# Two hand-over terms and a new table of priority shifts in a kernel's own list scheduler

## The chip, the cores and the metric

The kernel runs on one NeuronCore of a Trainium2 chip. That core has a matrix engine (TensorE, PE in the profile, with its weight loads as PEld), a vector engine (VectorE, DVE), a scalar engine (ScalarE, ACT), GpSimd (POOL) and SyncE (SP), whose queue issues the loads from HBM. The engines run their own instruction streams in order and wait for each other by semaphores. The metric is the device time of one execution in microseconds; the kernel before takes 958.61 us, the median of three runs (958.48 to 958.99).

## The reference

Three stages follow each other. `q`, `k` and `v` are 4 × 8 × 576 × 64 (batch, heads, sequence, width); the tokens are 2304 rows of 512.

```python
# attention: two softmax attentions, summed
q_d, k_d, v_d = (mean over 4 neighbouring positions of q, k, v)   # 144 positions
out_d = softmax(scale * q_d @ k_d.T) @ v_d                         # then each row repeated 4 times
attn  = softmax(where(|i - j| < 4, scale * q @ k.T, -1e9))         # a band of 7 keys
x     = out_up + attn @ v                                          # -> (2304, 512)
# moe
h = x @ w_in                                # 512 -> 2048
g = maximum(h, 0) + alpha * minimum(h, 0)
x = g @ w_out                               # 2048 -> 512
# moe2
xn  = x / sqrt(mean(x*x) + 1e-6) * rms_g
g   = xn @ w_gate                           # 512 -> 1536
out = (g * sigmoid(g) * (xn @ w_val)) @ w_out2   # 1536 -> 512
```

Weights and `alpha`, `rms_g` arrive as float64, that is as pairs of 32-bit words.

## The kernel before, in words

**Products.** Every float32 factor of the large products is split into two float16 parts, `split` (L414): ScalarE writes the high part (L415), VectorE the low part (L416), after scaling with powers of two. A product is three float16 matmuls.

**Weights.** A `Piece` is a part of a weight. For each of its two halves SyncE loads the word pairs into a tile `wr` (L1143 for `w_in`, L1153 for `w_out`; a half of `w_in` is 768 KB), and `decode` (L1158) makes float32 of it: ScalarE works on the high words (L1162) and, for some pieces, on the low words (L1165), and VectorE joins them into `wc` or `wo` (L1167, or L1170 and L1171). `square` takes sums of squares on TensorE (L1183 `sqps`) and VectorE (L1184); from those of the first three pieces of `w_in`, six halves, `scale_in` makes the scale `swi` by a sum over the partitions (L391 `allps`) and some small steps. Only then can the first `wi<-wc,swi` (L415), a split of `w_in`, run, and the first product of the MoE after it.

**Batch 0's attention**, class `Dense`, works on four pairs of heads. `load` (L788) issues q and k of a head pair, two DMAs each (L795), 144 KB apiece; `loadv` (L803) and `vwin` (L815) bring v. `tr` transposes q and k on TensorE (L844 `tps`), ScalarE copies the result to `T` (L845; `T_185`, `T_190`, `T_200` and `T_205` are the head pairs 0 to 3), VectorE adds up neighbours (L847). `down` is the downsampled attention (scores L867, exponentials L877, transposes L895, copies `aT` L896, product L904, copies `outd` L909), `local` the banded one in thirds of the sequence ("lanes" 0, 1, 2): scores L920 to L932, exponentials L952, their normalizing L959 to L967, transposes L976 with copies `laT` L978, product L988, and a split to `xt`, the MoE's input. Lane 0 must be through before the MoE starts; lanes 1 and 2 run beside it.

**The first MoE product.** `m1_first` takes lanes 0, 1, 2 (192 columns each) over 16 blocks of `w_in` in pairs: `h_mm` (L1409) multiplies (L1416 `hps`), ScalarE takes the negative part (L1420 `g`), VectorE applies alpha (L1422), and the result is split (L415 and L416 with `g<-hps,sc`). Lane 0 also splits `w_in` on the way, so ScalarE has much to do there. Lane 1's attention and the decoding of `w_out` are woven between these steps. The remaining 700 us are long rows of matmuls: `acc` (L1433), `gps` (L1533), `oacc` (L1562).

**The order.** `issue_order` (L56) sets each engine's order. It holds a model of the machine: `cost` and `transfer` give durations, `lag` the delay from the end of an instruction to the start of one that needs it, and a flag `slow` says whether TensorE runs at half clock at that point of the model. A list scheduler, run 40 times backward and forward, gives each instruction a priority `lead`. Then every entry of `LEADS`, (from, to, shift in ns), shifts the priorities of a range of instruction numbers; a last forward run with these gives the order, which is fixed by `add_manual_dep`. The DMAs go out on one queue of SyncE, in its order.

## Time and profile before

| | |
|---|---|
| median of the runs | 958.61 us |
| the profiled execution's own time | 958.69 us |
| its span in the profile | 957.0 us |
| TensorE busy | 928.3 us, 97% |
| VectorE busy | 676.8 us, 71% |
| ScalarE busy | 481.4 us, 50% |
| GpSimd busy | 128.0 us, 13% |
| moved by DMA | 73.79 MB, mean 77 GB/s |

The span runs from the first to the last instruction that the profiler sees, and some 1.7 us of the execution lie around it. TensorE is busy nearly throughout; its idle time lies almost all in the first 100 us. In that part the other engines and the loads have their densest work.

### The profile page before, as it was taken

How to read it: one execution, taken by the hardware profiler on the slowest of the kernel's cores; microseconds unless marked ns; L12 is line 12 of the kernel's file. 1: busy time of each engine (PE TensorE's matmuls, PEld its weight loads, DVE VectorE, ACT ScalarE, POOL GpSimd, SP SyncE). 2: the span in 40 equal slices, each digit the busy share in tenths (PEclk: the TensorE clock that was granted, in tenths of full speed). 3: DMA queues.
4: the chain of work that ended last, by engine and by line, in shares of the span. 5: the costliest groups of instructions: out<-in, count | busy, mean ns of one | idle time of the engine just before them, and what ended most of it. 6: DMA issues, size and time to landing. Idle time of an engine off the chain costs nothing.

```text
span 957.0 us, 16449 instructions
## 1 busy us (share of the span) xinstructions
PE 928.3 (97%) x6484; PEld 599.6 (63%) x6484; DVE 676.8 (71%) x1333; ACT 481.4 (50%) x1108; POOL 128.0 (13%) x103
## 2 busy tenths in 40 slices
PE   6978999999999999999999999999999999999998
PEld 5667877799555565556666655555566666555554
DVE  4789996899999968999977899973333342442333
ACT  5899989889872472233576322222332433221322
POOL 1101100211022003332102323220000000000000
PEclk9999999999999999999999999999999999999999
DMA  9976444574221241121032120200000000000000
GB/s 214 278 253 177 130 143 130 196 234 137 72 74 58 91 150 50 55 78 55 25 88 84 50 65 20 50 18 1 23 12 1 1 2 1 1 1 12 23 1 34
DMA packets 53711, 73.79 MB, mean 77 GB/s; under 512 B 22190, under 2 KB 35138, under 8 KB 53634
## 3 DMA queue, kind: packets, MB, share of 16 engines
q1 hardware_dynamic: 53634, 72.74, 25.3%
q8 instruction: 51, 0.84, 0.4%
q14 instruction: 26, 0.21, 0.1%
HBM read 68.01 MB, written 4.72 MB: 76 GB/s over the span
## 4 chain that ended last, share of the span: by engine, by line
PE 78%; ACT 4%; DMA 3%; DVE 3%; issue 1%; SPq 0%; ACTq 0%
PE gps L1533 26%; PE acc L1433 16%; PE hps L1416 16%; PE oacc L1562 14%; DMA out_dram<-ob 3%; PE avps L749 1%; PE sps L709 1%; PE atps L737 1%; DMA wr<-in_moe_w_gate_dram 1%; ACT wr L1165 1%; ACT w L415 1%; DVE prod L575 1%; PE xps L612 1%; DVE hps L1422 1%; DVE wc L1167 0%
## 5 line engine op out<-in xcount | busy, mean ns | idle before, releaser
L1416 PE MATMUL hps<-xt,wi 128*128 128x192 f16 (+1 forms) x1536 | 345.9, 289 | 6.6 <-DVE g L416 4.3
L1533 PE MATMUL gps<-x,w 128*128 128x384 f16 x1728 | 349.5, 326 | 0.6 <-ACT x L1447 0.4
L1433 PE MATMUL acc<-ghl,wo 128*128 128x384 f16 (+1 forms) x960 | 249.4, 310 | 0.5 <-ACT ghl L415 0.4
L1533 PEld LDWEIGHTS <-w 128*128 128x128 f16 x1728 | 169.4, 98 | 116.5 <-issue 2.6
L1562 PE MATMUL oacc<-w,uhl 128*128 128x512 f16 x630 | 200.4, 379 | 1.8 <-ACT ob L1618 1.7
L1416 PEld LDWEIGHTS <-wi 128*128 128x128 f16 x1536 | 148.0, 100 | 59.3 <-issue 7.7
L1433 PEld LDWEIGHTS <-wo 128*128 128x128 f16 x1344 | 128.8, 99 | 60.0 <-issue 2.6
L1422 DVE SCALAR_TENSOR_TENSOR hps<-g,oma,hps 128x192 f32<-128x192 f32 (+1 forms) x128 | 66.1, 517 | 66.1 <-ACT g L1420 65.4
L1542 ACT ACTIVATE th<-gps,tsc 128x384 f32<-128x384 f32 x72 | 41.7, 581 | 124.2 <-PE gps L1533 123.9
L1562 PEld LDWEIGHTS <-uhl 128*128 128x128 f16 x630 | 61.8, 98 | 64.3 <-issue 2.5
L1544 DVE SCALAR_TENSOR_TENSOR th<-th,gps 128x384 f32<-128x384 f32 x72 | 39.6, 551 | 84.9 <-ACT th L1542 84.7
L1553 ACT ACTIVATE uhl<-gps 128x384 f16<-128x384 f32 x72 | 41.7, 579 | 107.0 <-DVE gps L1547 98.5
L1420 ACT ACTIVATE g<-hps 128x384 f32<-128x384 f32 x96 | 47.0, 489 | 95.7 <-PE hps L1416 95.4
L521 POOL TENSOR_TENSOR prod<-cq,ckv 128x896 f32<-128x896 f32 x24 | 53.1, 2213 | 172.9 <-DVE ls L532 52.2
L1433 PE MATMUL acc<-g,wo 128*128 128x384 f16 (+1 forms) x384 | 69.8, 286 | 0.0
L1554 DVE TENSOR_TENSOR uhl<-gps,uhl 128x384 f16<-128x384 f32 x72 | 45.4, 630 | 28.4 <-ACT uhl L1553 28.1
L575 POOL TENSOR_TENSOR prod<-ls,ckv 128x896 f32<-128x896 f32 x24 | 47.9, 1997 | 126.4 <-issue 54.8
L416 DVE SCALAR_TENSOR_TENSOR ghl<-hps,grp,ghl 128x384 f16<-128x384 f32 (+1 forms) x73 | 44.3, 608 | 27.0 <-ACT ghl L415 26.7
L415 ACT ACTIVATE ghl<-hps,grp 128x384 f16<-128x384 f32 (+1 forms) x73 | 41.9, 574 | 40.2 <-DVE hps L1422 37.2
L532 DVE TENSOR_REDUCE ls<-prod 128x14 f32<-128x896 f32 x48 | 51.0, 1076 | 0.0
L1162 ACT ACTIVATE wr<-wr 128x768 f32<-128x768 f32 (+1 forms) x48 | 41.5, 874 | 8.7 <-DMA wr<-in_moe_w_val_dram 4.9
L1547 DVE SCALAR_TENSOR_TENSOR gps<-th,kap,gps 128x384 f32<-128x384 f32 x60 | 37.1, 618 | 9.6 <-PE gps L1533 7.0
(240 smaller groups left out, 1143.4 us busy)
## 6 DMA issues: line engine op xcount, KB each, us to landing
wr<-in_moe_w_out_dram SPq DMA_DIRECT2D x18, 512.0 KB
wr<-in_moe_w_in_dram SPq DMA_DIRECT2D x10, 768.0 KB
wr<-in_moe_w_gate_dram SPq DMA_DIRECT2D x8, 768.0 KB
wr<-in_moe_w_val_dram SPq DMA_DIRECT2D x8, 768.0 KB
ckv<-in_k_dram SPq DMA_DIRECT2D x7, 768.0 KB
ckv<-in_v_dram SPq DMA_DIRECT2D x7, 768.0 KB
wr<-in_moe_w_out_dram SPq DMA_DIRECT2D x20, 256.0 KB
sd<-in_q_dram SPq DMA_DIRECT2D x24, 144.0 KB
```

The lines of the kernel that those rows point to most:

```text
L415: nc.scalar.activation(out=hi, in_=src, func=AF.Copy, scale=s)
L416: nc.vector.scalar_tensor_tensor(out=lo, in0=src, scalar=s, in1=hi, op0=ALU.mult, op1=ALU.subtract)
L521: engs[i].tensor_tensor(out=pr, in0=view(st["q"][:, j, t:t + TP], [[D, TP], [0, ND], [1, D]]), in1=view(st["k"][:, j, t:t + TP], [[D, TP], ...
L532: nc.vector.tensor_reduce(out=st["s"][:, j, t:t + TP], in_=st.pop(("p", i)), axis=AX.X, op=ALU.add)
L575: engs[i].tensor_tensor(out=over(pr, i), in0=view(st["s"][:, j, t:t + TP], [[ND, TP], [1, ND], [0, D]]), in1=view(st["v"][:, j, t:t + TP], ...
L1416: nc.tensor.matmul(ps[:, j], wi[:, f + j, a, kk * 128:(kk + 1) * 128], x[:, b_, kk, c0:c0 + n], start=(i == 0), stop=(i == 3 * KK - 1))
L1420: nc.scalar.activation(out=g, in_=ps, func=AF.Relu, scale=-1.0)
L1422: nc.vector.scalar_tensor_tensor(out=ps[:, j], in0=g[:, j], scalar=oma[:, f + j:f + j + 1], in1=ps[:, j], op0=ALU.mult, op1=ALU.add)
L1433: nc.tensor.matmul(acc[e], wo_f(f)[:, a, e * 128:(e + 1) * 128], hl[:, b_], start=(f == f0 and i == 0), stop=(f == f1 and i == 2))
L1533: nc.tensor.matmul(ps, w2_t[i0 + f // 3].rearrange("p a (k c) -> p a k c", k=KK)[:, a, kk, (f % 3) * 128:(f % 3 + 1) * 128], xh[:, b_, kk] ...
L1554: nc.vector.tensor_tensor(out=t1, in0=vp, in1=t0, op=ALU.subtract)
L1562: nc.tensor.matmul(acc[tt], t[:, a, tt * 128:(tt + 1) * 128], w[:, b_, f % 3], start=(f in first and i == 0), stop=(f in last and i == 2))
```

## The change

Three terms of the model change, and the table. In `transfer`, a load of at most 16 runs takes at least 3000 ns. In the forward run, while `slow` is set, a TensorE instruction that found its engine idle costs 90 ns more, and whatever waits for a TensorE instruction gets it 100 ns later (`late`). The table `LEADS` is another one, of 159 shifts in place of 164. No instruction is added or taken away on any engine: the two orders are permutations of the same instructions. Behind the changed lines all line numbers are larger by 3 (L845 becomes L848).

```diff
--- before.py
+++ after.py
@@ -22,34 +22,33 @@
 
 
 LEADS = (
-    (6142, 6149, 8500), (4634, 4657, 4000), (1841, 1850, 500), (2437, 2444, -500), (1116, 1482, 1000), (6896, 6972, -500),
...
+    (1516, 1525, -4500), (5545, 5548, 22500), (6896, 6972, -500), (6862, 6881, -3000), (3753, 3934, -5500), (1566, 1613, 500),
...
@@ -113,7 +112,7 @@
         n = max(runs(a)[0] for a in (o, i))
         each = 4.0 * min(runs(a)[1] for a in (o, i))
         share = n / 16 * (10.0 + 0.046 * each)
-        return max(share, n / rings * (9.0 + 0.042 * each)), max(share, 600.0)
+        return max(share, n / rings * (9.0 + 0.042 * each), 3000.0 if n <= 16 else 0.0), max(share, 600.0)
 
     def cost(k, ins, outs):
         i, e = insts[k], eng[k]
@@ -253,11 +252,15 @@
                 k = heapq.heappop(soon[e])[1]
                 heapq.heappush(now[e], (prio[k], k))
             k = heapq.heappop(now[e])[1]
+            late = 0.0
             if fwd and e == "PE":
                 while t >= (win + 1) * WIN:
                     slow, win, done = done < BUSY, win + 1, 0
                 done += work[k]
                 real[k] = (2 * d[k] - 2.5 if slow else d[k]) + fixed[k]
+                if slow:
+                    real[k] += 90.0 if t > clock[e] else 0.0
+                    late = 100.0
             if fwd and shared[k]:
                 real[k] += max(0.0, port - t)
                 port = t + real[k]
@@ -266,7 +269,7 @@
             seq[e].append(k)
             for s in S[k]:
                 left[s] -= 1
-                at[s] = max(at[s], end[k] + (lag(k, s) if fwd else lag(s, k)))
+                at[s] = max(at[s], end[k] + late + (lag(k, s) if fwd else lag(s, k)))
                 if not left[s]:
                     if fwd and mate.get(k) == s:
                         heapq.heappush(now[e], (-1e30, s))
```

What that does to the order, at three places.

SyncE's queue, from the sixth load of k to behind the last one. `wo<-in_q_dram` and `wo<-in_k_dram` are loads of batch 0's q and k, `wr<-in_moe_w_in_dram` a half of a piece of `w_in`, `sdv` and `vw` are v. Before:

```order
L795 DMA wo<-in_k_dram 96x6x64
L1143 DMA wr<-in_moe_w_in_dram 128x2x768
L795 DMA wo<-in_k_dram 96x6x64
L795 DMA wo<-in_q_dram 96x6x64
L815 DMA vw_186<-in_v_dram 93x64
L815 DMA vw_186<-in_v_dram 96x3x64
L1143 DMA wr<-in_moe_w_in_dram 128x2x768
L795 DMA wo<-in_k_dram 96x6x64
L815 DMA vw_186<-in_v_dram 6x4x64
L815 DMA vw_186<-in_v_dram 96x4x64
L815 DMA vw_186<-in_v_dram 6x4x64
L1143 DMA wr<-in_moe_w_in_dram 128x2x768
```

After:

```order
L798 DMA wo<-in_k_dram 96x6x64
L806 DMA sdv<-in_v_dram 72x2x512
L1146 DMA wr<-in_moe_w_in_dram 128x2x768
L798 DMA wo<-in_q_dram 96x6x64
L806 DMA sdv<-in_v_dram 72x2x512 x2
L1146 DMA wr<-in_moe_w_in_dram 128x2x768
L818 DMA vw_186<-in_v_dram 93x64
L798 DMA wo<-in_k_dram 96x6x64
L818 DMA vw_186<-in_v_dram 96x3x64
L818 DMA vw_186<-in_v_dram 6x4x64
L1146 DMA wr<-in_moe_w_in_dram 128x2x768
```

The last k load here is that of head pair 3. It had four halves of `w_in` ahead of it in the queue, two of them further up than these rows; now it has six, four of them further up, and these six are all that the first scale needs.

ScalarE, around the copies `T_205` of head pair 3 (`aT` and `laT` are copies of transposed probabilities, `dls` and `dd` probabilities). Before:

```order
L967 ACTIVATE dls<-dls,dlsum 96x102
L896 ACTIVATE aT<-atps 72x288
L1162 ACTIVATE wr<-wr 128x768
L967 ACTIVATE dls<-dls,dlsum 96x102
L1165 ACTIVATE wr<-wr,nhalf 128x768
L896 ACTIVATE aT<-atps 72x288 x2
L978 ACTIVATE laT<-ltps 102x384
L845 ACTIVATE T_205<-tps 128x288
L1162 ACTIVATE wr<-wr 128x768
L845 ACTIVATE T_205<-tps 128x288
L896 ACTIVATE aT<-atps 72x288
```

After:

```order
L970 ACTIVATE dls<-dls,dlsum 96x102 x6
L880 ACTIVATE dd,dsum<-sps,dm 72x144 x3
L970 ACTIVATE dls<-dls,dlsum 96x102
L880 ACTIVATE dd,dsum<-sps,dm 72x144
L848 ACTIVATE T_205<-tps 128x288 x2
L970 ACTIVATE dls<-dls,dlsum 96x102
L1165 ACTIVATE wr<-wr 128x768
L981 ACTIVATE laT<-ltps 102x384
L848 ACTIVATE T_205<-tps 128x288
L899 ACTIVATE aT<-atps 72x288
L848 ACTIVATE T_205<-tps 128x288
```

Before, the first three `aT` stood ahead of the first `T_205`; now the first comes behind three of the four. The transposes on TensorE that give `aT` (L895) moved in the same way: 22 small matmuls that stood ahead of the transposes of head pair 3's k, 16 of L895, four of L904, one each of L391 and L976, now stand behind.

ScalarE, up to the first split of `w_in` (`wi<-wc,swi`). Before:

```order
L415 ACTIVATE xt<-dxs,sc 128x192
L1165 ACTIVATE wr<-wr,nhalf 128x768
L978 ACTIVATE laT<-ltps 102x384
L1162 ACTIVATE wr<-wr 128x768
L1165 ACTIVATE wr<-wr,nhalf 128x768
L415 ACTIVATE xt<-dxs,sc 128x192
L1162 ACTIVATE wr<-wr 128x768
L415 ACTIVATE wi<-wc,swi 128x512 x9
L1162 ACTIVATE wr<-wr 128x768
L1420 ACTIVATE g<-hps 128x384
```

After:

```order
L418 ACTIVATE xt<-dxs,sc 128x192
L1165 ACTIVATE wr<-wr 128x768
L1168 ACTIVATE wr<-wr,nhalf 128x768
L418 ACTIVATE xt<-dxs,sc 128x192
L1165 ACTIVATE wr<-wr 128x256
L955 ACTIVATE dls,dlsum<-lsps,dlm 96x102 x14
L418 ACTIVATE wi<-wc,swi 128x512 x2
L955 ACTIVATE dls,dlsum<-lsps,dlm 96x102 x2
L418 ACTIVATE wi<-wc,swi 128x512 x4
L1165 ACTIVATE wr<-wr 128x768
```

Fourteen of the 16 exponentials of lane 1 (`dls,dlsum<-lsps`), of which thirteen stood behind the first nine splits and the rest further on, now stand ahead of the first split, and so do three decodes of high words of `w_out` (one 128x768, two 128x256), which stood behind it.

## Rows read from the trace of the kernel before

**Rows 1.** Busy time by stretch (start:end, length; per engine busy and instructions; PEclk; DMA; GB/s)
```profile
0.00:35.00 35.00, 25.89 (x161) 20.01 (x162) 19.71 (x67) 21.71 (x67) 4.67 (x29) 1.00 1.00 227
35.00:62.02 27.02, 25.37 (x199) 18.46 (x198) 20.51 (x48) 25.03 (x73) 2.43 (x2) 1.00 0.72 247
62.02:96.00 33.98, 27.32 (x294) 24.06 (x295) 31.84 (x77) 33.84 (x82) 3.99 (x8) 0.90 0.71 222
96.00:225.00 129.00, 127.71 (x1358) 107.23 (x1356) 113.79 (x272) 116.17 (x288) 16.55 (x13) 1.00 0.52 162
225.00:957.00 732.00, 721.98 (x4480) 429.86 (x4479) 490.93 (x872) 284.67 (x603) 100.33 (x52) 1.00 0.14 42
```

**Rows 2.** ScalarE's waits, 0 to 62.02 us (total us, times, longest us)
```profile
ACT T L845 <- PE tps L844: 9.9, 5, 5.5
ACT wr L1162 <- DMA wr<-in_moe_w_in_dram: 1.7, 1, 1.7
ACT aT L896 <- PE atps L895: 1.6, 4, 0.7
```

**Rows 3.** ScalarE by line and shape, 0 to 110 us (busy us, mean ns; idle before)
```profile
L1162 ACT ACTIVATE wr<-wr 128x768 f32<-128x768 f32 x20 | 18.1, 910 | 1.9 <-DMA wr<-in_moe_w_in_dram 1.7
L952 ACT ACTIVATE dls<-lsps,dlm 96x102 f32<-96x102 f32 x48 | 15.8, 343 | 0.3 <-DVE dlm L938 0.2
L1165 ACT ACTIVATE wr<-wr,nhalf 128x768 int32<-128x768 uint32 x14 | 14.0, 999 | 0.0
L415 ACT ACTIVATE wi<-wc,swi 128x512 f16<-128x512 f32 x16 | 10.5, 718 | 0.3 <-DVE swi L406 0.3
L978 ACT ACTIVATE laT<-ltps 102x384 f32<-102x384 f32 x8 | 3.8, 495 | 0.0
```

**Rows 4.** SyncE's queue in order of time (start us, us issuing)
```profile
25.86 1.36 SPq L795 DMA_DIRECT2D wo<-in_k_dram  x1
```

**Rows 5.** DMA, 0 to 36 us: rate in 40 slices, total, issues
```profile
GB/s 0 0 181 237 243 203 213 184 340 357 261 188 232 252 255 232 249 192 185 176 224 199 204 241 254 244 257 260 201 158 242 312 284 221 152 190 309 325 402 397
DMA packets 12547, 8.33 MB, mean 231 GB/s; under 512 B 10491, under 2 KB 10511, under 8 KB 12544
wr<-in_moe_w_in_dram SPq DMA_DIRECT2D x6, 768.0 KB
```

**Rows 6.** TensorE in order of time, 20 to 62 us (start us, us, idle before)
```profile
27.84 1.27 PE L895 MATMUL atps<-ident,dd 72*72 72x72 f32 x7
...
34.63 1.01 PE L844 MATMUL tps<-ident,wo 96*128 96x96 f32 x5
...
35.57 1.23 PE L904 MATMUL avps<-aT,dd 72*64 72x144 f32 x8
...
60.62 0.38 PE L391 MATMUL allps<-s,ones 128*128 128x3 f32 x2 [1.04 <-DVE sqps L1184]
```

**Rows 7.** ScalarE in order of time, 62.01 and 86 to 88 us
```profile
62.01 1.33 ACT L415 ACTIVATE wi<-wc,swi 128x512 f16<-128x512 f32 x2 [0.34 <-DVE swi L406]
...
86.71 0.49 ACT L1420 ACTIVATE g<-hps 128x384 f32<-128x384 f32 x1
87.08 0.59 ACT L415 ACTIVATE g<-hps,sc 128x384 f16<-128x384 f32 x1
```

**Rows 8.** TensorE in order of time, 88 to 94 us
```profile
88.38 0.57 PE L1416 MATMUL hps<-xt,wi 128*128 128x192 f16 x5 [0.16 <-DVE g L416]
...
89.05 0.55 PE L988 MATMUL lops<-laT,vw 102*64 102x96 f32 x8
...
93.63 0.60 PE L932 MATMUL lsps<-T 64*96 64x102 f32 x8
```

**Rows 9.** Busy time by stretch after the first weight split's start
```profile
64.40:67.80 3.40, 3.40 (x22) 3.13 (x23) 3.40 (x6) 3.26 (x7) 0.00 (x0) 0.50 1.02 382
74.70:78.10 3.40, 3.40 (x27) 3.26 (x25) 2.63 (x5) 3.40 (x16) 0.00 (x0) 0.50 0.98 292
...
88.40:125.00 36.60, 35.31 (x417) 29.28 (x417) 35.06 (x97) 34.20 (x109) 4.59 (x9) 1.00 0.48 136
```

53 rows, old and new, of the table LEADS are left out of this document.

## The prediction

> **What bounds the kernel now.** I read the table of stretches first. From 225 us to the end TensorE is busy for 722.0 of 732.0 us, from 96 to 225 us for 127.7 of 129.0 [rows 1]: there the kernel can't get shorter by order, save for a microsecond or two. The open time is ahead of 96 us: TensorE idles 9.1 us of the first 35, 1.7 of the next 27 and 6.7 of the 34 after that. So the question is by when the first 96 us have handed their work to TensorE, which from then on pays any lateness in full at the end.
>
> In those 96 us I then asked who is late. Between 62.02 and 96 us it is ScalarE: busy 33.84 of 33.98 us, while TensorE is at 27.3 [rows 1]. At 88.38 us the fifth pair of MoE products starts right behind VectorE's half of a split (0.16 us of idle), and that split ran on ScalarE at 87.08 us [rows 7, 8]: ScalarE, then VectorE, then TensorE. From 88.4 to 125 us TensorE still idles 1.3 us in all [rows 9]. So ScalarE's stream up to the split at 87.08 us sets the time, and everything ahead of it on ScalarE counts, work and idle time alike.
>
> Ahead of 62.02 us ScalarE is not full: it worked 21.7 + 25.0 = 46.7 us and idled 15.3. The waits name the reasons: copies of transposed q and k that wait for TensorE (9.9 us), the first word pairs of `w_in` (1.7 us), and copies of transposed probabilities (1.6 us) [rows 2]. The first split of `w_in` at 62.01 us waits only for its scale (0.34 us), which goes back to the sum over partitions on TensorE at 60.62 us [rows 6, 7].
>
> **What the change does, part by part.** Nothing is added or removed, so each price is one of place.
>
> *The new terms of the model* cost no time on the chip; only the order does.
>
> *The loads of q and k behind those of `w_in`.* Two more halves of 768 KB, together 2 × 0.786 = 1.57 MB, go out ahead of the last k. Its predecessors were issued until 25.86 us [rows 4], and TensorE transposed this k in the main at 34.63 us [rows 6]. At 231 GB/s, the mean of the first 36 us, the 1.57 MB take 6.8 us; at 402 GB/s, the best slice, 3.9 us [rows 5]. I take 5.0 us (317 GB/s, the middle of the two rates), since the loads of long rows stand among the short ones: of the packets in this stretch, 10491 of 12547 are under 512 B [rows 5]. TensorE shows no wait for this load now, so its cover is used up at 34.63 us and the delay counts whole: transposes at 39.6 us. The Trainium skill, "DMA: Bandwidth & Descriptors", section Specifications, puts the limit of HBM for one core at about 358 GB/s; the slices of 402 and 397 GB/s exceed it [rows 5]. By the page this term would be 4.4 us by estimate, 0.6 less.
>
> *22 small matmuls that stood ahead of those transposes stand behind them.* Sixteen of L895 at (1.27 − 0.33)/6 = 0.157 us each, 2.5 us; four of L904 at (1.23 − 0.46)/7 = 0.11, 0.4 us [rows 6] (0.33 and 0.46 are taken for the last one's length in such a row); two more at about 0.2. Together 3.4 us. If nothing else fills TensorE's wait for the load, they come on top of the delay; if they run in idle time that TensorE had anyhow, they are free. Both ends stay in the range; I take half, 1.7 us.
>
> *Up to the first split.* From TensorE's 34.63 us to the split at 62.01 us were 27.4 us, in which TensorE was busy for all but 1.7 of 27 [rows 1]; I keep that length. The split then comes at 39.6 + 27.4 + 1.7 = 68.7 us (67.0 to 70.4 by the matmuls alone, 65.9 to 72.2 with both ends of the rate).
>
> *Work that ScalarE now does ahead of the first split.* Fourteen exponentials of lane 1, at 15.8/48 = 0.33 us each, 4.6 us; one decode of 128x768, 18.1/20 = 0.9 us, and two of 128x256 at about half of it [rows 3]. That is 6.4 us by sums of busy time; as neighbours overlap by about 0.1 us (87.08 − 86.71 = 0.37 us between a start and the next where the first lasts 0.49 [rows 7]), I take 6.0. It falls into ScalarE's idle time as long as there is some: up to the split ScalarE has 46.7 + 6.0 = 52.7 us of work, so it idles 68.7 − 52.7 = 16.0 us, against 15.3 before. The cover of these 6 us is thus the wait for the scale; without the late loads the idle time would be down at 9.3 us, and that difference is the whole intended gain.
>
> *The balance at the split that was at 87.08 us.* Ahead of it ScalarE has, in the new order, four copies `laT` more (3.8/8 = 0.475 each, 1.9 us), four splits of `w_in` (10.5/16 = 0.656, 2.6), two decodes of low words (1.0 each) and half a one (0.5), one decode of high words and a half one (0.9 + 0.45), one split of `xt` (0.45), and one negative part less (0.49) [rows 3, 7]. That is 8.3 us by busy time; with the same overlap over some twelve instructions, 7.2. These 7.2 us contain the 6.0 of before, shifted inside. So that split comes 7.2 + (16.0 − 15.3) = 7.9 us later.
>
> *What TensorE has done by then.* It too has more behind it: sixteen products L988 (0.12 each by the pitch of 0.48 us for four instructions, which the row counts as eight [rows 8], 1.9 us), eight scores L932 (two rows of 0.52, 1.05), twelve sums of squares at 0.067 us (0.8), four transposes and four mask products (0.7): 4.4 us, which stood behind 88.38 us before and needn't be done there again. And of the 1.3 us that TensorE idled from 88.4 to 125 us [rows 9] a later stream would pay nothing. Lateness at the end: 7.9 − 4.4 − 1.3 = **+2.2 us**.
>
> *The rest of the order*, up to some 750 us, is shuffled too. TensorE idles 1.3 us from 96 to 225 us and 10.0 behind that [rows 1], much of it at the kernel's end, where the order is the same as before. A wait taken away can give back a part of it and a new one can add the like; the trace doesn't show the new waits. I put it at zero, with 1 us to either side, worked out from the 1.3.
>
> **Sum.** The profiled execution took 958.69 us by its own time, 957.0 in its span; that is 0.08 us above the median. 958.69 + 2.2 = **960.9 us**. This case's own range goes with the split from 65.9 to 72.2 us: −0.6 to +5.7 us, 958.1 to 964.4.
>
> **Rivals.** The measurement can tell 0.2%, 1.9 us, from no change.
>
> *The holes fill (faster).* ScalarE's five waits for transposes, 9.9 us [rows 2], are just where the new order puts three decodes of `w_in`. If the queue of loads shares its rate out so that k is late by half of what I take (2.5 us), and the 22 matmuls run in idle time, the split comes at 62.0 + 2.5 = 64.5 us, ScalarE's idle time is 64.5 − 52.7 = 11.8 us, and the sum is 7.2 + 11.8 − 15.3 − 4.4 − 1.3 = −2.0: 956.7 us. With no delay at all the idle time is 9.3 and the sum −4.5: 954.2. It decides from a split ahead of about 64.6 us. For it: TensorE idles 9.1 us in the first 35 [rows 1], so its stream has room early on. Against it: the loads run without a gap to 36 us [rows 5], and the last k can't overtake 1.57 MB for nothing.
>
> *They cancel (same).* With the split between 64.6 and 68.4 us the sum stays within 1.9 us: 958.7 us at 66.5. For it: the ends of the two unknown terms lie on both sides.
>
> *The decodes stop the queue (slower).* ScalarE is in order: a decode that waits for its load stops the copies behind it, and TensorE's next matmuls with them. Before, this was one wait of 1.7 us [rows 2]. In the new order the first five decodes of `w_in` all come within the first copies and ahead of lane 0's exponentials; three more waits of 1.0 us each (half to two thirds of the one seen) on top of my case give an idle time of 19.0 us, +5.2: 963.9 us.
>
> *TensorE's clock.* Two stretches of 3.4 us at 64.4 and 74.7 us ran at a granted clock of 0.50, that is at 1.2 of 2.4 GHz, TensorE busy throughout [rows 9]; just ahead of each it had been idle for much of the time. Each can cost up to 1.7 us. If the products start later and closer together, one or both may go (down to −3.4 us, 957.5 from my case); a third would add 1.7 (962.6). The Trainium skill, "TensorE: Matmul & The Clock Gate", section What's actually happening, says that the throttled state is the default and that activity releases it. The two rows agree with that in so far as they follow idle time; by it a denser stream from 66 us on would lose these stretches. It doesn't alter my sum, since ScalarE sets the pace there.
>
> **How the numbers follow.** My case 0.34, the stopped queue 0.14, cancelling 0.24, filled holes 0.28; the clock moves each of them by its 1.7 us either way and has no share of its own. So faster 0.28, same 0.24, slower 0.48. The likeliest is 960.9 us. The range leaves out about a tenth on either side: below, the part of the filled holes with next to no late load (under 955.2), above, what lies over 964.4. It is 955.2 to 964.4 us.
>
> **What would show it.** Right: the five transposes of the last k at 38 to 41 us instead of 34.63; the first split of `w_in` at 66 to 72 us; ScalarE busy 52 to 53 us up to there; the fifth pair of products near 96 us instead of 88.38; TensorE then as full as before. Wrong: a first split ahead of 64.6 us (then faster), ScalarE idle behind the first split (then the balance at 87.08 us doesn't hold), waits for `w_in` of over 3 us on ScalarE (then the stopped queue), more or fewer stretches at half clock, or a change in TensorE's idle time behind 125 us of over 1 us.

## The result, and the profile after

The changed kernel takes 972.32 us (median of six runs, 968.03 to 976.28) against 959.74 for the kernel before (six runs, 958.48 to 961.64): a ratio of 1.0125, with a 95% interval of 1.0101 to 1.0149. The forecast, 960.9 us, had the sign and not the size, and the time lies outside its range. The profiled execution took 971.18 us by its own time, 969.5 in its span: 12.5 us more than the profiled one of before in either. One run of a kernel further down, e4, had a mean granted clock of 0.95 and took 1002.11 us; the time given for e4 leaves it out. Line numbers are larger by 3 from here on.

The table of stretches of the kernel after, in the columns of [rows 1]; the last two rows are for use further down:

```profile
0.00:35.00 35.00, 19.52 (x116) 14.49 (x117) 18.05 (x54) 21.12 (x64) 3.23 (x28) 1.00 1.03 241
35.00:62.02 27.02, 24.44 (x171) 17.62 (x168) 18.38 (x44) 18.97 (x60) 5.43 (x3) 1.00 0.71 223
62.02:96.00 33.98, 26.98 (x280) 22.32 (x277) 28.13 (x71) 33.95 (x86) 4.46 (x8) 1.00 0.71 215
96.00:225.00 129.00, 125.66 (x1336) 104.41 (x1336) 111.75 (x267) 114.05 (x288) 16.40 (x12) 1.00 0.48 151
225.00:969.00 744.00, 731.11 (x4591) 439.08 (x4589) 495.64 (x900) 292.46 (x615) 101.88 (x52) 1.00 0.14 44
...
400.00:500.00 100.00, 96.83 (x606) 58.76 (x606) 92.45 (x163) 39.86 (x95) 28.66 (x13) 1.00 0.19 60
...
0.00:74.33 74.33, 53.98 (x361) 39.74 (x362) 44.58 (x124) 52.37 (x169) 9.90 (x33) 1.00 0.87 231
```

Take TensorE's idle time, length less busy time, row by row, and before's from [rows 1] off it: 15.5 − 9.1 = 6.4 us more in the first 35 us, 2.6 − 1.7 = 0.9 in the next 27, 7.0 − 6.7 = 0.3 up to 96 us, 3.3 − 1.3 = 2.0 up to 225 us and 13.4 − 10.0 = 3.4 behind (the row ends 0.47 us ahead of the span's end at 969.47, and TensorE is idle in that rest). Together that is 13.05 us more idle time; TensorE is busy 0.56 us less in all (927.71 against 928.27), which leaves the 12.5 us. Half of it is lost in the first 35 us, where ScalarE also had less done (21.12 against 21.71 us) and in the next stretch much less (18.97 against 25.03). The last row is ScalarE's stretch up to the first split of `w_in`, which now starts at 74.33 us and not at 62.01 [rows 7]: busy 52.37 us, idle 21.96.

What ScalarE waited for up to that split (total us, times, longest us):

```profile
ACT T L848 <- PE tps L847: 8.9, 3, 6.0
ACT wr L1165 <- DMA wr<-in_moe_w_in_dram: 7.0, 6, 2.4
ACT outd L912 <- PE avps L907: 2.9, 2, 2.5
ACT aT L899 <- PE atps L898: 1.7, 4, 0.7
```

Against [rows 2] the copies of q and k wait 1.0 us less, the decodes of `w_in` wait six times instead of once, 5.3 us more, and the copies `outd` of the downsampled attention's result, which before show no wait, 2.9 us. ScalarE in order of time (start us, us, idle before and what ended it):

```profile
9.61 0.90 ACT L1165 ACTIVATE wr<-wr 128x768 f32<-128x768 f32 x1 [0.78 <-DMA wr<-in_moe_w_in_dram]
...
14.38 0.90 ACT L1165 ACTIVATE wr<-wr 128x768 f32<-128x768 f32 x1 [2.42 <-DMA wr<-in_moe_w_in_dram]
...
20.24 0.90 ACT L1165 ACTIVATE wr<-wr 128x768 f32<-128x768 f32 x1 [1.50 <-DMA wr<-in_moe_w_in_dram]
...
45.65 0.29 ACT L912 ACTIVATE outd<-avps 128x144 f32<-128x144 f32 x1 [2.53 <-PE avps L907]
...
74.33 1.36 ACT L418 ACTIVATE wi<-wc,swi 128x512 f16<-128x512 f32 x2
```

Each of these decodes stands ahead of a copy of q or k; behind the second of them TensorE's next transposes wait 1.15 us for that copy. The split at 74.33 us has no idle time in front: from 53 us on ScalarE had only one wait, of 0.7 us. So nearly all of its idle time lies ahead of 53 us, and from there on only its work counts.

VectorE does the same with the other end of a decode. It joins the words at 27.00 us, having waited 1.38 us for them, and only then takes the step that TensorE waits for:

```profile
27.00 0.96 DVE L1170 SCALAR_TENSOR_TENSOR wc<-wr 128x768 int32<-128x768 int32 x1 [1.38 <-ACT wr L1168]
...
28.33 0.27 DVE L400 TENSOR_REDUCE sc<-rowps 1x1 f32<-1x128 f32 x1
```

TensorE in order of time: the products that wait for that step, the last k, and the sum for the scale:

```profile
28.65 0.58 PE L402 MATMUL colps<-sc,ones 1*128 1x1 f32 x2 [3.22 <-DVE sc L400]
...
38.03 0.55 PE L847 MATMUL tps<-ident,wo 96*128 96x96 f32 x2 [0.61 <-DMA wo<-in_k_dram]
...
71.71 0.58 PE L394 MATMUL allps<-s,ones 128*128 128x3 f32 x2 [0.89 <-DVE sqps L1187]
```

Of TensorE's waits up to the split only those for q are longer in all (3.8 us) than the 3.22 us of the first row. The last k is transposed at 38.03 us against 34.63, and the sum for the scale runs at 71.71 against 60.62 [rows 6]: 3.4 us late there, 11.1 here. So more is lost behind the last k than ahead of it. Its load was issued at 26.02 us, about when it was before (25.86 [rows 4]), and landed 11.88 us later.

The fifth pair of products, which the forecast had near 96 us and which was at 88.38 before [rows 8]:

```profile
101.87 0.49 PE L1419 MATMUL hps<-xt,wi 128*128 128x192 f16 x4 [0.33 <-DVE g L419]
```

### The profile page after: what moved, and what is told of

The parts are those of the page before. It is cut to its first block, busy times and chain, and to the rows that moved or that the text cites. A ratio compares the mean times of both kernels' runs of the same rounds, so it can differ in the third digit from the quotient of the medians.

```text
span 969.5 us, 16449 instructions
## 1 busy us (share of the span) xinstructions
PE 927.7 (96%) x6484; PEld 597.9 (62%) x6484; DVE 672.0 (69%) x1333; ACT 480.5 (50%) x1108; POOL 131.4 (14%) x103
## 4 chain that ended last, share of the span: by engine, by line
PE 79%; DVE 7%; ACT 6%; DMA 6%; issue 1%; SPq 1%; ACTq 0%; POOL 0%; DVEq 0%; POOLq 0%
PE gps L1536 27%; PE acc L1436 16%; PE hps L1419 16%; PE oacc L1565 13%; DMA wr<-in_moe_w_in_dram 2%; DMA out_dram<-ob 1%; DMA wo<-in_k_dram 1%; ACT wr L1165 1%; ACT wi L418 1%; PE sps L712 1%; PE avps L752 1%; DVE w L419 1%; DVE prod L578 1%; ACT wr L1168 1%; DMA sd<-in_q_dram 1%
## 5 line engine op out<-in xcount | busy, mean ns | idle before, releaser
L1419 PE MATMUL hps<-xt,wi 128*128 128x192 f16 (+1 forms) x1536 | 351.9, 286 | 7.1 <-DVE g L419 3.3
L1536 PE MATMUL gps<-x,w 128*128 128x384 f16 x1728 | 345.3, 326 | 2.3 <-DVE ghl L419 1.5
L1565 PE MATMUL oacc<-w,uhl 128*128 128x512 f16 x630 | 196.9, 379 | 1.4 <-ACT ob L1621 1.4
L1547 DVE SCALAR_TENSOR_TENSOR th<-th,gps 128x384 f32<-128x384 f32 x72 | 39.6, 552 | 93.6 <-ACT th L1545 93.1
L524 POOL TENSOR_TENSOR prod<-cq,ckv 128x896 f32<-128x896 f32 x24 | 56.2, 2342 | 159.0 <-DVE ls L535 53.4
L1436 PE MATMUL acc<-g,wo 128*128 128x384 f16 (+1 forms) x384 | 74.2, 286 | 0.0
```

Source lines behind the costliest of these rows:

```text
L524: engs[i].tensor_tensor(out=pr, in0=view(st["q"][:, j, t:t + TP], [[D, TP], [0, ND], [1, D]]), in1=view(st["k"][:, j, t:t + TP], [[D, TP], ...
L1419: nc.tensor.matmul(ps[:, j], wi[:, f + j, a, kk * 128:(kk + 1) * 128], x[:, b_, kk, c0:c0 + n], start=(i == 0), stop=(i == 3 * KK - 1))
L1436: nc.tensor.matmul(acc[e], wo_f(f)[:, a, e * 128:(e + 1) * 128], hl[:, b_], start=(f == f0 and i == 0), stop=(f == f1 and i == 2))
L1536: nc.tensor.matmul(ps, w2_t[i0 + f // 3].rearrange("p a (k c) -> p a k c", k=KK)[:, a, kk, (f % 3) * 128:(f % 3 + 1) * 128], xh[:, b_, kk] ...
L1565: nc.tensor.matmul(acc[tt], t[:, a, tt * 128:(tt + 1) * 128], w[:, b_, f % 3], start=(f in first and i == 0), stop=(f in last and i == 2))
```

## The experiments

All kernels are the changed one with a function behind its planner that permutes the orders of single engines: `after` is the new order of each engine, `before` the old one (planned with the old model and table), `end` the model's end of each instruction in ns. Four theories are named by letters in the expectations. L: the late loads of q and k cost the time, by their places in SyncE's queue. W: the decodes of `w_in` cost it, which wait in ScalarE's order for their loads and hold up the copies behind. W2, which took W's place after the first four runs: a load, its decode, its join and the buffer that it frees belong together, and moving one alone makes another wait. P: the price lies in the places of the instructions as a whole, and stays when those loads are gone.

### Early and late part apart

```diff
 first = {k for k in count if end[k] <= LIMIT}
-seq = after
+seq = {e: [k for k in after[e] if k in first] + [k for k in before[e] if k not in first] for e in after}
```

That is e1 with a limit of 67.7 us and e5 with 110 us; e2 and e6 take the first part from `before` and the rest from `after`, with 58 and 110 us by the old model's ends.

> All that the new scheduler model ends ahead of the first split of w_in stands in the new order, all the rest in the old one. Both parts are the full work. Theory A (the loss is made ahead of the first split, on the way to it): close to the changed kernel, 969 to 974 us, first split at 73 to 75 us. Theory B (the shuffled order behind it makes a good part): TensorE's idle time behind 96 us falls back by some 4.9 us to that of before, so 965 to 968 us. Theory C (all of it lies behind): 959 us.

> The other way round: the old order up to the first split of w_in, the new one for all the rest. Theory A: 958 to 961 us, first split at 62 us. Theory B: 962 to 965 us. Theory C: 970 to 973 us.

> The new order for all that its model ends ahead of 110 us, the old one behind that; at this seam the two orders hold nearly the same set of instructions (ScalarE differs in 4, VectorE in 6, TensorE in 22), which the seam at the first split did not. Theory A (the loss is made in the first 110 us): 968 to 974 us. Theory B (the later order has a share of its own, some 4.9 us, of TensorE's idle time): 964 to 968 us. Theory D (each half loses only beside the other): 958 to 962 us.

> The other way round, old order up to 110 us of its model, the new one behind. Theory A: 958 to 961 us. Theory B: 962 to 966 us, with TensorE idle some 3 to 5 us more behind 110 us than before. Theory D: 968 us or more in spite of an early part like that of before.

Measured: e1 971.58 us (ratio 1.0129, 1.0082 to 1.0176), e5 970.64, e2 973.66, e6 968.33. The new early part alone gives about the whole loss. The later part put behind the old early one loses too, and in e2 a part of it is the seam's own: at 69.75 us ScalarE waited 6.06 us for a load of `w_in` whose decode came early by one order and whose load late by the other. So these four don't share the loss out between the parts; the stretch from 400 to 500 us does that better. Before, then e5 (old late part), then e6 (new late part), each to be held against the row of after above:

```profile
400.00:500.00 100.00, 99.02 (x644) 61.96 (x643) 89.96 (x170) 47.47 (x119) 22.12 (x11) 1.00 0.22 64
```

```profile
62.02:96.00 33.98, 27.65 (x263) 22.51 (x264) 27.47 (x69) 33.95 (x91) 4.78 (x9) 0.71 0.71 224
...
400.00:500.00 100.00, 99.02 (x613) 60.02 (x612) 95.22 (x167) 39.32 (x90) 28.74 (x14) 1.00 0.19 59
```

```profile
400.00:500.00 100.00, 97.08 (x611) 58.95 (x610) 92.11 (x165) 41.05 (x100) 28.09 (x13) 1.00 0.19 60
```

TensorE is busy 99.0 us there in every profile with the old late part (before, e1, e5, e8, e10, e12, e15) and 96.2 to 97.8 in every one with the new (after, e2, e3, e6, e7, e9, e11, e13, e14, e16, e17, e18), however late the kernel runs. The later order thus costs some 2 us by waits of its own: TensorE's products `hps` wait 2.2 us for VectorE's split `ghl` in this stretch after, 0.9 before, and 0.7 us for `th`, which before shows no wait.

### The loads, the decodes, and both

e3 puts the first 34 entries of SyncE's queue into the old order. e4 keeps the new loads and has the first five decodes of `w_in` and four of their joins further back, behind the copies that they held up. e7 does both. e8 is the old order throughout with the new order of the first 31 entries of SyncE's queue.

```diff
-seq = after
+seq = dict(after, SP=sorted(after["SP"][:34], key=before["SP"].index) + after["SP"][34:])    # e3, e7
+move(seq, "Activation", (430, 431), 136); ... ; move(seq, "DVE", (432,), 164); ...           # e4, e7
+seq = dict(before, SP=sorted(before["SP"][:31], key=after["SP"].index) + before["SP"][31:])  # e8
```

(`move` puts the instructions of the given numbers right behind another on their engine.)

> The changed kernel, only the first 34 loads in the order that the kernel before has them in: k and q ahead of the halves of w_in, as before; all compute engines keep the new order. Theory L (the loads of k behind two more halves of w_in are what costs, as the prediction has it): most of the early loss returns, 962 to 966 us, last k transposed near 35 us. Theory W (ScalarE and VectorE stop at decodes of w_in placed too early, and all that stands behind them waits): the halves of w_in land later still and the decodes stand where they stood, so no gain or a loss, 971 to 980 us, with ScalarE's waits for w_in above the 7.0 us of the changed kernel.

> The changed kernel, only the first five decodes of w_in on ScalarE, and the first four joins on VectorE, moved behind the next group of attention work that stood behind them (copies T, exponentials); loads, TensorE and GpSimd as changed. Theory W: ScalarE's waits for w_in fall from 7.0 us to under 2.5, TensorE idles some 4 to 6 us less in the first 35, 964 to 968 us. Theory L: the transposes of k come as late as now, 970 to 973 us.

> Both edits at once: the first 34 loads in the old order and the first five decodes of w_in behind the next attention work; each edit alone made it slower. Theory W2 (loads and decodes must come in step: a decode ahead of its load stops ScalarE, a load ahead of the free buffer, which the late decode holds, stops SyncE's queue and the k and q behind it): both waits fall, ScalarE's for w_in under 3 us and TensorE's for q and k under 5 us, 962 to 968 us. Theory P (the order of TensorE's own work is what costs): still 971 us or more, with other waits in their place.

> The kernel before, with only its first 31 loads in the new order, halves of w_in first. Theory W2: ScalarE's decodes come late, so the third half of w_in waits for its buffer and holds up q and k behind it: TensorE waits some 5 to 10 us for q and k, 966 to 974 us. Theory L (only the bytes ahead of k count): the last k comes 5 us later, 961 to 964 us.

Measured: e3 977.07 us (ratio 1.0178, 1.0150 to 1.0205), e4 974.35, e7 975.09, e8 968.42 (964.7 to 972.8; ratio 1.0100, 1.0059 to 1.0142). ScalarE's waits in e3:

```profile
ACT wr L1165 <- DMA wr<-in_moe_w_in_dram: 15.5, 3, 6.5
ACT T L848 <- PE tps L847: 8.2, 3, 5.6
```

With q and k early again the kernel got 5 us slower, not faster: the decodes now wait 15.5 us, and TensorE's transposes wait 9.8 us for the copies behind them. The last k, though its load stands early again, is transposed at 45.33 us. So the places of these loads alone, L, are not the reason, and W's mechanism is there. But W's remedy fails: with the decodes moved back (e4, e7) nothing is won. TensorE's waits in e7:

```profile
PE tps L847 <- DMA wo<-in_k_dram: 6.1, 1, 6.1
PE tps L847 <- DMA wo<-in_q_dram: 5.0, 2, 2.9
PE colps L402 <- DVE sc L400: 4.5, 1, 4.5
```

The late decodes keep their buffers longer, the loads that need these stand in SyncE's queue, and the q and k behind them are late: 11.1 us of waits in place of those removed (SyncE's load of `w_in` waits 2.4 us for a join in e7, and 6.0 us in e8). e8 shows the other side. The new loads alone, on the old order of the rest, cost 9.5 us (968.42 against 958.92 beside it), by longer waits; the one for `alpha`, a small table behind the loads, was 1.0 us before:

```profile
PE vecps L1701 <- DMA rows<-in_moe_alpha_dram: 5.6, 1, 5.6
PE tps L847 <- DMA wo<-in_k_dram: 3.8, 1, 3.8
PE tps L847 <- DMA wo<-in_q_dram: 3.5, 1, 3.5
```

That is what W2 forecast for e8; its 962 to 968 us for e7 it missed by 7.

### The same with three loads left out

In these four the second halves of the first three pieces of `w_in`, 2.36 MB, aren't loaded; GpSimd writes zeros in their place. The order is fixed: that of after in e9, of before in e10, the new one up to 110 us and then the old in e15, the reverse in e16.

```diff
-for rows, x in srcs:
+for rows, x in srcs if not (w is w_in and half and self.c0 < 3*UC) else ():
...
+nc.gpsimd.memset(r.bitcast(F32), 0.0)
```

> The new order on all engines, but the second halves of the first three pieces of w_in are not loaded; GpSimd sets their tiles to zero (so this leaves out 2.36 MB of early loads; all later work is done). Theory W (what the new order loses early, it loses to w_in landing late for decodes that stand early): ScalarE's waits for w_in fall from 7.0 us to under 2, first split of w_in ahead of 68 us, 962 to 966 us; what remains against the kernel before is the later order. Theory P (the order of the compute work itself is worse): 969 us or more.

> The same with the order of the kernel before, as the measure for the run without these loads. Theory W: the old order waits for w_in little (1.7 us), so it gains little: 956 to 959 us, and the new order is 4 to 8 us behind it rather than 12.6. Theory P: 956 to 959 us, and the new order stays 11 us or more behind.

> Without the three early loads: new order up to 110 us of its model, old one behind. The runs without these loads vary less (969.3 and 958.9 us for all new and all old). Theory B (the later order costs 2 to 4 us by itself): 965.5 to 967.5 us. Theory A (only the first 110 us count): 968.5 to 970 us.

> The other way round, without the three early loads: old order up to 110 us, new one behind. Theory B: 961 to 963 us. Theory A: 958 to 960 us. Above 964 us the two parts would not add up.

Measured, with the ratio to the kernel before run beside each on the same chip (the runs of this study were spread over several, on which before had medians from 957.8 to 960.3 us): old and old (e10) 958.93 us, 0.9985; new and old (e15) 967.37, 1.0089; old and new (e16) 965.89, 1.0067; new and new (e9) 969.33, 1.0097 (1.0064 to 1.0131). Without 2.36 MB of the early loads the new order still costs 10.4 us by the medians, 1.0097 − 0.9985 = 1.1% or 10.7 us by the ratios, out of 12.6 us with all loads. So the loads' bytes aren't the main price, as P says. The early part costs 8.4 us here (10.0 by the ratios), the later one 2.0 on top of it (0.8), but 7.0 by itself (7.9). The stretch behind the seam tells why, in e16 and then in e10:

```profile
96.00:125.00 29.00, 25.10 (x257) 19.01 (x253) 24.02 (x75) 25.14 (x89) 4.18 (x4) 0.88 0.54 143
```

```profile
96.00:125.00 29.00, 27.43 (x319) 22.59 (x314) 27.16 (x82) 26.27 (x93) 4.17 (x4) 1.00 0.50 142
```

In e16 TensorE idles 2.3 us more there, and its granted clock averages 0.88: some 7 us of the 29 were at the lower level, 1.2 GHz, worth up to 3.5 us. The changed kernel is at 1.00 there and idles 2.4 us, 0.8 more than e10. With 1.9 us more idle time from 400 to 500 us these make 7.7 of the 8.7 us between the two spans. So most of the 7.0 us belongs to the seam; that the clock's part counts in full is read off, not tried by itself.

### Moves of one or two steps

e11 puts the first load of `w_in` behind one k and one q, and the join that VectorE made at 27.00 us behind the steps for `colps`. e12 is e11 with the old order behind 110 us. e13 moves the two copies `outd` back. e14 is e11 and e13 together without the three loads. e11's changes on SyncE (first) and VectorE, and e13's on ScalarE:

```diff
-L1146 DMA wr<-in_moe_w_in_dram 128x2x768
-L798 DMA wo<-in_k_dram 96x6x64
-L798 DMA wo<-in_q_dram 96x6x64 x2
+L798 DMA wo<-in_k_dram 96x6x64
+L798 DMA wo<-in_q_dram 96x6x64
+L1146 DMA wr<-in_moe_w_in_dram 128x2x768
+L798 DMA wo<-in_q_dram 96x6x64
...
-L1170 SCALAR_TENSOR_TENSOR wc<-wr 128x768
 L1702 COPY rg<-vecps 128x4
...
 L415 TENSOR_SCALAR sc<-sc 128x1
+L1170 SCALAR_TENSOR_TENSOR wc<-wr 128x768
...
-L912 ACTIVATE outd<-avps 128x144
 L880 ACTIVATE dd,dsum<-sps,dm 72x144 x2
 L899 ACTIVATE aT<-atps 72x288
 L880 ACTIVATE dd,dsum<-sps,dm 72x144 x2
+L912 ACTIVATE outd<-avps 128x144
```

> The changed kernel with two single moves: the first half of w_in goes behind the last load of head pair 0's k on SyncE, and VectorE's fourth join of w_in goes behind the small steps for alpha that TensorE waits for. Full work. Theory W: TensorE's wait at the alpha step falls from 3.2 us to under 1, that for k from 2.5 to under 1; ScalarE's waits for w_in stay, so only a part returns: 966 to 970 us. Theory P: no gain, 971 to 974 us.

> The two moves, and behind 110 us of the model the old order. Theory B (the later order costs 3 to 4 us by itself, on top of whatever the early part loses): 2 to 4 us under the run with the two moves alone. Otherwise the same as that run.

> The changed kernel, only the two copies outd on ScalarE (2.9 us of waits for TensorE) moved behind the work that stood behind them. Full work. Theory I (what counts is ScalarE's idle time up to the first split, whatever it waits for): the split comes 1 to 3 us earlier than in the changed kernel, 969 to 971.5 us. Theory P (TensorE's own order sets the split): no change, 971.5 to 974 us.

> The new order without the three early loads (2.36 MB left out, their tiles set to zero), with the two moves of the earlier run and the copies outd later. Theory I: first split at 67 to 69 us in place of 71.8, time lower by 1.1 times that, 964 to 967 us against 969.3. Theory P: 968.5 to 970 us.

Measured: e11 971.89 us (ratio 1.0122), e12 972.45 (1.0122), e13 976.74 (1.0175, 1.0147 to 1.0202) and e14 969.28 (1.0097). e12 was to be 2 to 4 us under e11 and isn't; the two share their early order, and yet the last k is at 35.42 us in e11's profile, at 42.02 in e12's. In e11 the wait of `colps` fell from 3.2 to 1.4 us, but the median didn't move: now scores wait 3.3 us for copies of q and k. e13 only renamed its wait and got slower:

```profile
ACT wr L1165 <- DMA wr<-in_moe_w_in_dram: 10.9, 6, 2.6
...
ACT dd L880 <- PE avps L907: 2.6, 1, 2.6
```

The exponentials `dd` behind `outd` wait for the same products (2.6 us for 2.9). In e14 the load of `w_in` moved and its decode didn't: one wait of 4.8 us for it, and nothing won over e9.

### One half moved as a whole

e18 moves load, decode and joins of the first half together: on SyncE as e11, on ScalarE the decode's two steps behind the four copies of head pair 0, on VectorE its join with them, and the join at 27.00 us as in e11. e17 is the same without the three loads.

```diff
+move(seq, "SP", (428,), 30)
+move(seq, "Activation", (430, 431), 136)
+move(seq, "DVE", (432,), 164)
+move(seq, "DVE", (456,), 77)
```

> The new order without the three early loads (tiles set to zero), and the first half of w_in moved as a whole: its load behind head pair 0's k, its decode on ScalarE behind the copies of that k and its join on VectorE behind the work after it; the fourth join behind the small steps for alpha. The run that moved the load and not the decode stopped ScalarE once for 4.8 us. Theory W2 (load and decode must move together): that wait is under 1.5 us, the first split ahead of 70 us, 964 to 967 us. Theory P (TensorE's own order): 968.5 to 970 us.

> The same moves with all loads, full work. Theory W2: ScalarE's first wait for w_in under 1.5 us, TensorE's waits for k and at the alpha step under 2 us together, 967 to 970 us against 972.3. Theory P: 971 to 974 us.

Measured: e17 965.31 us (965.2 to 966.4; ratio 1.0077, 1.0061 to 1.0092) against 969.33 and 1.0097 of e9; e18 969.24 (ratio 1.0116, 1.0097 to 1.0136) against 972.32 and 1.0125 of the changed kernel. The medians fall by 4.0 and 3.1 us, as W2 expected. But before was 2 us faster beside them too, so by the ratios the gains are 1.9 and 0.9 us, within the intervals: the times alone don't prove them. The traces agree with W2 and don't prove it either, since each is one execution. ScalarE's waits in e18:

```profile
ACT T L848 <- PE tps L847: 10.1, 5, 5.7
ACT wr L1165 <- DMA wr<-in_moe_w_in_dram: 3.7, 5, 1.2
```

The decodes wait 3.7 us instead of 7.0, `colps` is no longer among TensorE's longest waits, and the first split comes at 72.09 us instead of 74.33. But e11's profile, with the load moved and its decode not, has it at 71.70, and e15's, with no move, shows waits of 0.3 us where e17 has 0.6 and e9 2.3. No kernel with all the loads beat the kernel before.

## Why the prediction was wrong, point by point

**What held.** The slower side; that ScalarE's stream sets the time (busy 33.95 of 33.98 us from 62 to 96 us); its work up to the first split (52.37 us, forecast 52.7); the last k (38.03 us, forecast 38 to 41). The last is luck in part: two more profiles of the same early order have it at 38.56 and 43.15 us (e1, e5), and waits that the sum left out moved it, as shown below. Two of the forecast's own signs of being wrong came: waits for `w_in` of 7.0 us on ScalarE, and a change in TensorE's late idle time, 3.4 us behind 225 us alone.

**The formula held for all but 4.3 us.** The forecast said: the end is late by 7.2 us of work on ScalarE, plus its idle time up to the first split less 15.3, less 4.4 that TensorE has done, less 1.3 that it idled. In spans: 957.0 + 7.2 − 15.3 − 4.4 − 1.3 = 943.2 us plus that idle time. Each row is one profile with the new early order or a variant of it (all such kernels but e4, whose profile is of the run left out above, and e2, whose seam lies ahead of the split). The work ahead of the split is nearly the same in all of them (51.8 to 52.6 us), so the idle time says the same as the time of the split; two columns part that time at the last k:

| kernel | late part | waits for `w_in`, us | last k, us | first split, us | from k to split | ScalarE idle up to split | span | span − (943.2 + idle) |
|---|---|---|---|---|---|---|---|---|
| e17 | new | 0.6 | 31.68 | 68.00 | 36.3 | 15.9 | 963.5 | 4.4 |
| e11 | new | 3.0 | 35.42 | 71.70 | 36.3 | 19.5 | 966.6 | 3.9 |
| e18 | new | 3.7 | 35.80 | 72.09 | 36.3 | 19.6 | 967.2 | 4.4 |
| e9 | new | 2.3 | 35.54 | 71.81 | 36.3 | 19.7 | 969.0 | 6.1 |
| e14 | new | 4.8 | 36.52 | 73.36 | 36.8 | 21.2 | 968.6 | 4.2 |
| after | new | 7.0 | 38.03 | 74.33 | 36.3 | 22.0 | 969.5 | 4.3 |
| e13 | new | 10.9 | 40.99 | 77.81 | 36.8 | 25.3 | 972.5 | 4.0 |
| e7 | new | 7.7 | 45.10 | 80.63 | 35.5 | 28.4 | 976.5 | 4.9 |
| e3 | new | 15.5 | 45.33 | 80.87 | 35.5 | 29.1 | 976.6 | 4.4 |
| e15 | old | 0.3 | 33.69 | 70.01 | 36.3 | 17.7 | 963.7 | 2.8 |
| e1 | old | 8.2 | 38.56 | 74.82 | 36.3 | 22.4 | 967.4 | 1.8 |
| e12 | old | 11.7 | 42.02 | 78.31 | 36.3 | 26.0 | 971.2 | 2.0 |
| e5 | old | 12.3 | 43.15 | 78.75 | 35.6 | 26.5 | 972.9 | 3.2 |

Over 13 us of idle time the span follows it one for one: the last column stays between 3.9 and 4.9 us with the new late part (e9 apart) and between 1.8 and 3.2 with the old.

**The step that failed: "I keep that length".** The forecast let the split follow the last k by the 27.4 us of before, with 1.7 us for the moved matmuls: 29.1 us. It was 36.3 us, 7.2 more. As the last k came 1.6 us earlier than forecast (38.03 for 39.6), the split was 5.6 us later than forecast and ScalarE's idle time up to it 22.0 us, not 16.0. These 6.0 us are more than half of the 10.3 us between the forecast's +2.2 and the 12.5 measured.

The length goes with the order of the compute engines and not with the loads. It is 35.5 to 36.8 us in all 13 rows of the table, and 27.4 or 27.5 us in the five profiles with the old early order on these engines (before, e6, e8, e10, e16). e8 and e3 cross the two: in e8 the compute engines have the old order and the loads the new one, in e3 the reverse. In both the last k is transposed at 45.3 us, and their splits are 8.2 us apart. The stretch from the last k to the split, in the columns of [rows 1], before, after, then e8, e3 and e17:

```profile
34.63:62.01 27.38, 25.74 (x202) 18.83 (x200) 20.58 (x48) 25.39 (x73) 2.43 (x2) 1.00 0.72 249
```

```profile
38.03:74.33 36.30, 32.03 (x230) 23.50 (x231) 24.56 (x64) 29.74 (x103) 5.54 (x4) 1.00 0.69 223
```

```profile
45.31:72.68 27.37, 25.79 (x202) 19.01 (x200) 20.58 (x48) 25.43 (x74) 2.43 (x2) 1.00 0.70 241
```

```profile
45.33:80.87 35.54, 30.35 (x232) 22.59 (x231) 24.60 (x64) 29.60 (x103) 6.13 (x5) 0.75 0.64 200
```

```profile
31.68:68.00 36.32, 32.03 (x232) 23.53 (x231) 24.56 (x64) 30.46 (x106) 6.50 (x5) 1.00 0.65 211
```

Half of the 8.9 us is work: ScalarE is busy 29.74 us in this stretch, before 25.39. The forecast put its 6.0 us of added work into the 15.3 us that ScalarE idled, but 13.3 of these lie ahead of the last k; behind it ScalarE was as full as TensorE, 25.03 of 27.02 us [rows 1]. In the changed kernel the 14 exponentials run from 69.84 to 74.33 us, right up to the split, whose scale was ready at 73.18. The other half is idle time, 6.56 us for 1.99. In it ScalarE waits 6.5 us for TensorE, before 1.5 (`aT` 1.1, `T` 0.4):

```profile
ACT outd L912 <- PE avps L907: 2.9, 2, 2.5
ACT T L848 <- PE tps L847: 1.9, 1, 1.9
ACT aT L899 <- PE atps L898: 1.7, 4, 0.7
```

TensorE had done 3.6 us less when the last k came (busy 21.95 us up to there, before 25.52): of the 7.0 us that it idled more ahead of the last k, 3.4 show in the time of that k, and 3.6 come due behind it. It is so in e17 too (21.77), where TensorE idles little more than before. That is the size of the 22 matmuls, 3.4 us, of which the forecast took half. No run puts them or the exponentials back by themselves, so how the 8.9 us share out among the moved instructions stays open. The two `outd` copies alone aren't it: with them moved (e13, e14) the length is 36.8 us.

**The waits for `w_in`** are the mechanism of the rival of the stopped queue, priced there at three waits of 1.0 us; there were six, of up to 2.4 us, 5.3 us more than before. The order showed five decodes within the first copies, and each could have been given a landing time from the rate of [rows 5]; I took the one wait of [rows 2] as the size of a wait instead. But all six lie ahead of the last k, so they are part of its 38.03 us and not of the length behind it. Over the table the last k comes the later, the longer they are: at 31.7 and 33.7 us with waits of 0.6 and 0.3 us (e17, e15), at 45.3 with 15.5 (e3); e7 stands apart, where TensorE itself waits for q and k. Nor would their absence have brought the old split back: e17 and e15 have the last k earlier than the kernel before (34.63), and split at 68.00 and 70.01 us, where e10, the old order on the same loads, splits at 60.63. That ScalarE idles 15.9 us in e17, the forecast's 16.0, is chance: a last k 7.9 us earlier than the forecast's and a length 7.2 us longer.

**The remaining 4.3 us** lie behind the fifth pair of products, which started 13.5 us late (101.87 for 88.38; the formula with the measured idle time says 13.9). TensorE then had 5.3 us less to do than before (busy 852.0 us from there on, before 857.3; forecast 4.4 less), but it idled 15.6 us instead of 11.3: 13.5 − 5.3 + 4.3 = 12.5. The forecast had taken 1.3 us off for idle time that needn't be paid, and put the later order at 0 with 1 us to either side. Measured are 0.9 us more idle time from the fifth pair to 225 us, 1.5 more from 225 to 400, 2.2 more from 400 to 500 and 0.3 less behind. Only the third is a steady price of the later order; from 225 to 400 us the profiles with the new late part idle between 2.1 and 4.2 us, before 2.7.

**The clock.** The two stretches of [rows 9] are gone: 1.00 from 62 to 96 us, against 0.90 [rows 1]. I had allowed up to 3.4 us for that. It gave nothing that can be seen, as the sum said, since ScalarE sets the pace: e5, with the same early order, ran at 0.71 in that stretch (its row is above), at 1.2 GHz from some 61 to 80 us, and is only some 1.3 us above e1 and e12 in the last column; e3, at 0.70 there, is level with after, and in neither was the length from the last k to the split longer for it. The clock of e5 fell in a stretch, 60 to 62 us, in which TensorE was busy for 0.65 of 2 us; the changed kernel, busy for 1.81 there, stayed at 1.00. The Trainium skill, "TensorE: Matmul & The Clock Gate", section What's actually happening, has activity release the throttle; the two stretches agree with that in kind.

**What stays open.** e17 is free of most waits for `w_in`, and its span is still 963.5 − 957.0 = 6.5 us longer than that of before. By the table that is 0.6 us of idle time, the forecast's own balance of 7.2 − 5.7 = 1.5, and the 4.4 of the last column. Which of the moved instructions an order would have to put back to get the length behind the last k down to 27.4 us, no run tried; nor whether more buffers for `w_in` would let the decodes be where the order wants them.

## What to carry to other kernels

A length between two landmarks that is kept from one order to the next is a statement about every engine that works in it. Here [rows 1] showed that ScalarE had only 2 us of room in it, and the order put more than 4 us of work there: before work is credited to idle time, look on which side of the landmark that idle time lies. A landmark also parts causes: up to the last k the loads and the waits for them decide, behind it the order of the compute engines, and two kernels that cross the orders (e3, e8) tell which is which.

An instruction that waits for a load, put early into an in-order queue, can cost all that stands behind it the wait: give each early decode a landing time from the measured rate, and add up the waits, before pricing a new order. Moving a load, its decode or its join without the others gained nothing that can be told from noise in five kernels (e3, e4, e7, e11, e14) and lost up to 5 us; one half moved as a whole (e17, e18) gained 1 to 2 us by the ratios, which isn't clear of noise either. A stretch that sits far behind the disputed one, compared at the same place over many variants, can price the later part of an order when cutting the order in two can't, since the cut makes waits of its own.

## What had not been expected of the hardware

The same loads land at different times. The first decode of `w_in` of the kernel after started at 9.61 us, 0.78 us after ScalarE was free for it; in e5, whose order is the same up to there, and in e6, which starts as the kernel before does:

```profile
10.96 0.89 ACT L1165 ACTIVATE wr<-wr 128x768 f32<-128x768 f32 x1 [2.30 <-DMA wr<-in_moe_w_in_dram]
```

```profile
13.15 0.88 ACT L1165 ACTIVATE wr<-wr 128x768 f32<-128x768 f32 x1 [3.33 <-DMA wr<-in_moe_w_in_dram]
```

Before, that decode waited 1.7 us [rows 2]. The loads vary by 1.3 to 1.7 us here, and an order with six decodes in the way seems to suffer more from that than one with a single such wait: the new early order's waits for `w_in` ranged from 7.0 to 12.3 us in three profiles of it (after, e1, e5), its last k from 38.03 to 43.15 us, its first split from 74.33 to 78.75 us, and the kernel's time from 968.0 to 976.3 us, against 958.5 to 961.6 beside it before. What makes the landing vary, no trace here shows; e1 and e5 ran on different chips, so a part may be the chip's.
